# Bucketed attention into a rational feed-forward layer: sums and bits moved to stand ahead of a pair's first values product, and the other steps of a pair put at new places

## The chip, the cores and the metric

One core of one Trainium2 chip runs the whole program in one launch. The metric is the device time of that core in microseconds (us).

## The reference

Attention over 4 batches x 8 heads, 768 tokens, 64 wide, in which a query sees only the keys of its own bucket (six sign bits of a projection); then a feed-forward layer with a rational activation over the 3072 tokens of 512 features. All data is float32.

```python
q_bits = (einsum('bhsd,dk->bhsk', q, proj) > 0)           # k_bits likewise
mask = q_bucket[:, :, :, None] == k_bucket[:, :, None, :]
scores = np.where(mask, scale * q @ k.T, -1e9)
attn = exp(scores - max(scores)); attn = attn / (sum(attn) + 1e-09)
x = (attn @ v)  ->  [3072, 512]
h = x @ w_in                                              # [3072, 2048]
g = (a0 + a1*h + a2*h**2 + a3*h**3) / (1 + |b0|*|h| + |b1|*h**2 + 1e-6)
out = g @ w_out
```

## The kernel before

The 32 heads are worked in 16 pairs (NPAIR), p = 0 to 15; a pair stands on 128 partitions, two heads of 64. A product at near-float32 precision is made from two float32r matmuls: an operand is split into a rounded high part and the rest, the low part. After the pairs comes the feed-forward layer (`Ffn`), from about 406 us to the end, which the change hardly touches.

A pair has these steps; the name in brackets is that of its tile, as the profile and the order print it.

- `high`, `low` (q, k; lo): ScalarE rounds the operand, VectorE subtracts to get the low part. The low part has one buffer for q and one for k (`lo0`, `lo1`). `high_move`, `second_low` and `second_high` are SyncE's DMAs that lay the parts out for the scores.
- `bits` (psb): for two pairs at once, sixteen matmuls of 32 columns give the projections; VectorE takes the signs into `mb`, `penalties` scales them on ScalarE, `maskrows` moves them by four DMAs into spare rows of q and k, so that the scores' matmul itself adds the mask.
- `maxstep` (psm, m): for each of 12 blocks of rows a first product for the row maximum, two matmuls of 384 columns, which VectorE reduces. There are two PSUM buffers for it, which `bits` also uses.
- `shift_turn` (pst, mt) and `shift_rows`: the maxima are transposed and moved into one more row of q.
- `scores(p, s)` (pss, E): step s = 0 to 11. For each of two heads two matmuls into one PSUM tile, and ScalarE's exp into E. There are seven buffers E and three PSUM buffers of tag `s`, which psu and pst also use, in turn. GpSimd adds the E of three steps into `acc`, of which there are five.
- `values(p, s)` (psv): E times v, 64 columns to a head, accumulated over six steps in one PSUM buffer of tag `v`, which `values_out` copies out by ScalarE (col, xo). In pairs 1 to 14 the products of six steps are issued as one group of 24 matmuls, twice in a pair; in pair 15 in groups of 8.
- `sums` (psu, sr): sixteen matmuls of 32 columns on the four `acc` give the row sums, ScalarE copies them; `sums_store` and `recips` bring them through DRAM.
- `weights(i)`: loads and splits a block of the layer's weights (wr, ws, wi_hi, wi_lo), one of w_in and one of w_out in every pair; `tokens.load` makes the layer's first input block.

The order is written out ahead of time: `at(p, s, f, ...)` puts a step at place 12 p + s, the plan is sorted by place, and the instructions are issued in that order; nothing reorders them later, so that each engine's queue follows it. Work for pair p + 2 runs during pair p. The places of the middle pairs stand in the table `MID`, those of pair 0 and of what leads to it in `FIRST`. A place sets the order only; the time comes from the queues. The maxima of pair p + 2 are spread from place `maxima` + `maxima_steps` of pair p on (from pair p's step 7 to step 6 of pair p + 1).

Of the kernel before, what the change touches and what calls it, by code (L numbers as in the profile page):

```python
# [25 lines left out]
NPAIR = B * NHP  # L26
# [12 lines left out]
ACCS = 5  # L39

MID = dict(
    group=6, group_ends=2, values=[0.66, 0.05], values_ends=1.3, values_out=3.5, maxima=7.17,
    maxima_steps=[0, 1.15, 1.73, 2.64, 3.32, 5.08, 5.86, 6.98, 8.0, 8.84, 10.26, 11.37], sums=14.65, sums_store=17.37,
    high=[-0.41, 1.19], low=[1.06, 3.35], bits=2.81, penalties=4.05, high_move=1.9, maskrows=5.61, second_low=-2.2,
    second_high=2.69, load_v=10.99, shift_turn=8.61, shift_rows=8.82, load=9.0, recips=[20.0, 22.0, 23.0],
    weights=[[1.44, 4.0, 4.1, 5.09, 5.49, 7.11, 9.5, 9.75, 17.5], [8.05, 10, 10.65, 11.5, 12.38, 14.29, 16.34, 19.32, 21.22]],
    weights_last=[0.5, 0.8, 1.0, 1.2],
)

FIRST = dict(  # L50
    maxima0=[-0.28, 0.26, 1.25, 2.5, 2.92, 4.02], maxima1=4.13, rate1=0.48, maxima2=9.7, rate2=0.76,
    high=[1.64, 5.08], low=[3.52, 5.72], bits=5.52, penalties=7.05, high_move=7.01, maskrows=8.53, second_low=-0.75,
    second_high=7.95, load_v=9.81, shift_turn=9.64, shift_rows=9.65, group=2,
    values=[1.25, 1.5, 1.2, 0.57, 0.5, 0.94], values_out=1.96, high1=[7.05, 7.28], low1=[13.35, 22.75],
    high_move1=16.35, load2=10.64, load3=4.45, penalties1=0.83, maskrows1=4.05, first_shift=5.33,
    weights=[[0.71, 3.21, 4.75, 6.91, 11.35, 16.66, 25.25, 30.08, 32.02], [7.34, 8.03, 10.23, 11.08, 12.57, 13.45, 14.88, 21.36, 28.13]],
)
# [33 lines left out]
def bucket_attention_then_rational_ffn(ctx, tc, qT, kT, v, proj, w_in, w_out, coef, consts, out):  # L91
# [55 lines left out]
    def operands_to_terms():  # L147
        early.close()
        ffn.terms_pool(right)

    last = attention(tc, nc, raw, ps_b, tail, tokens, early, operands_to_terms, ffn, load, QF, KF, v, w_in, w_out, wo_d, ident, cst,
                     ones, prj, wi_hi, wi_lo, x_d, s_d, r_d, coefficients)
    ffn.rest(ctx, last)
# [3 lines left out]
def attention(ctx, tc, nc, raw, ps_b, tail, tokens, early, operands_to_terms, ffn, load, QF, KF, v, w_in, w_out, wo_d, ident, cst, ones, prj,  # L157
# [210 lines left out]
    def recips(bb):  # L368
        n = 2 * NHP * S // P
        s = tail.tile([P, n], F32, tag="rs", name=f"rs{bb}")  # L370
        nc.sync.dma_start(s, s_d[bb].rearrange("h (x c) -> (h x) c", c=n))
        yield
        z = tail.tile([P, n], F32, tag="rz", name=f"rz{bb}")
        d = tail.tile([P, n], F32, tag="rd", name=f"rd{bb}")
        r = tail.tile([P, n], F32, tag="rr", name=f"rr{bb}")
        nc.vector.tensor_scalar(out=z, in0=s, scalar1=0.0, scalar2=S * TINY, op0=ALU.is_equal, op1=ALU.mult)
        nc.vector.tensor_scalar(out=d, in0=s, scalar1=0.0, scalar2=1e-9, op0=ALU.is_gt, op1=ALU.mult)
        nc.vector.tensor_tensor(out=d, in0=s, in1=d, op=ALU.add)
        nc.vector.tensor_tensor(out=d, in0=d, in1=z, op=ALU.add)
        nc.vector.reciprocal(out=r, in_=d)  # L380
        yield
        nc.sync.dma_start(r_d[bb].rearrange("h (x c) -> (h x) c", c=n), r)
        yield
# [45 lines left out]
    def at(p, s, f, *args):  # L429
        plan.setdefault(12 * p + s, []).append((f, args))  # L430

    def spread(p, steps, gen):
        for s in steps:
            at(p, s, lambda g: next(g, None), gen)

    for p in range(NPAIR):
        mid = 0 < p < NPAIR - 1
        n = MID["group"] if mid else FIRST["group"] if p == 0 else MID["group_ends"]
        for s in range(12):
            at(p, s, scores, p, s)  # L440

            if p > 1:
                at(p - 2, MID["maxima"] + MID["maxima_steps"][s] if p > 2 else FIRST["maxima2"] + FIRST["rate2"] * s, maxstep, p, s)
            if s % n == n - 1:
                for i in range(s - n + 1, s + 1):
                    at(p, s + (MID["values"][s // n] if mid else FIRST["values"][s // n] if p == 0 else MID["values_ends"]), values, p, i)
            if s % NT == NT - 1:
                at(p, s + (MID["values_out"] if mid else FIRST["values_out"] if p == 0 else MID["values_ends"]+0.01), values_out, p, s // NT)
        for hf in range(2):
            at(p, 6 * hf + 9, values_store, p, hf)  # L450
        if p < NPAIR - 1:
            at(p, MID["sums"], sums, p)
            at(p, MID["sums_store"], sums_store, p)
        if p > 1:
            for t in range(2):
                at(p - 2, (MID if p > 2 else FIRST)["high"][t], high, p, t)
                at(p - 2, (MID if p > 2 else FIRST)["low"][t], low, p, t)
            if p % 2 == 0:
                at(p - 2, (MID if p > 2 else FIRST)["bits"], bits, p)
                at(p - 2, (MID if p > 2 else FIRST)["penalties"], penalties, p)  # L460
            at(p - 2, (MID if p > 2 else FIRST)["high_move"], high_move, p)
            at(p - 2, (MID if p > 2 else FIRST)["maskrows"], maskrows, p)
        if p > 0:
            at(p - 1, (MID if p > 1 else FIRST)["second_low"], second_low, p)
            at(p - 1, (MID if p > 1 else FIRST)["second_high"], second_high, p)
            at(p - 1, (MID if p > 1 else FIRST)["load_v"], load_v, p)
            at(p - 1, (MID if p > 1 else FIRST)["shift_turn"], shift_turn, p)
            at(p - 1, (MID if p > 1 else FIRST)["shift_rows"], shift_rows, p)
        if p > 3:
            at(p - 4, MID["load"], load, p)  # L470
        if p % NHP == NHP - 1 and p + 1 < NPAIR:
            spread(p, MID["recips"], recips(p // NHP))
# [5 lines left out]
        spread(0, [o + x for x in w], weights(i))  # L478

    for c in range(2):  # L480
        spread(NPAIR - 2, [9 * c + x for x in (6, 10, 11, 12)], tokens.load(0, c))
    at(NPAIR - 1, 2, operands_to_terms)
    for f in range(3):
        at(NPAIR, 2 + f, ffn.step, f)
    at(NPAIR, 2.5, sums, NPAIR - 1)

    load_v(0)
    warm(12)
# [241 lines left out]
```

## Time and profile before

| what | value |
|---|---|
| median of three runs | 951.18 us (950.34 to 953.0) |
| the profiled execution | 951.47 us, of which the span of its instructions 949.7 us |
| granted clock of TensorE | 0.998 |
| busy in the span | PE 938.9, VectorE 860.3, ScalarE 679.6, GpSimd 450.4 us |
| of that from 62 to 370 us (pairs 2 to 13) | PE 308.0 of 308.0, VectorE 270.9, ScalarE 215.4, GpSimd 246.1 us |

The matmuls are pipelined: one of 384 columns is shown as some 340 ns long, while the next one starts about 175 ns after it. So two of them cover each other, and a PE that is shown as always busy can still have lost time; this is read from the starts of the matmuls, or from the pieces of the chain of waits, which do not overlap. A score step (four matmuls) takes 0.70 us there, a block of maxima (two) 0.35 us.

### The profile page before, as it was taken

The numbers are of one execution on the slowest core, as the hardware profiler recorded it, in microseconds if no ns is written. First come the engines' busy times: TensorE is split into PE (matmuls) and PEld (weight loads), VectorE is DVE, ScalarE is ACT, GpSimd is POOL, SyncE is SP. The second block draws the span as 40 slices with busy tenths as digits, with TensorE's granted clock in tenths as the row PEclk, the third lists the DMA queues.
The fourth block names the chain that finished last, engine by engine and source line by source line (L and its number), as shares of the span: only waits on it lengthen the run. The fifth ranks groups of instructions, "written<-read, shape, count | busy, mean of one in ns | idle before, by whom it ended". The sixth has DMA issues, their size and how long they took to land.

```text
span 949.7 us, 14854 instructions
## 1 busy us (share of the span) xinstructions
PE 938.9 (99%) x5067; PEld 752.7 (79%) x5067; DVE 860.3 (91%) x1206; ACT 679.6 (72%) x1418; POOL 450.4 (47%) x399
## 2 busy tenths in 40 slices
PE   9999999999999999999999999999999999999998
PEld 5576767676767676488998998998998998998996
DVE  6789889888988897589999999999999999999996
ACT  6467777777777776777777777777777777777775
POOL 4377878787878787832222222222222222222222
PEclk9999999999999999999999999999999999999999
DMA  7568877778778777455121021021011110210000
GB/s 223 143 181 245 223 224 225 223 224 224 225 223 223 225 191 212 131 212 201 42 67 35 1 67 35 1 67 35 13 58 32 58 43 1 67 34 1 34 1 34
DMA packets 49888, 111.65 MB, mean 118 GB/s; under 512 B 9138, under 2 KB 21798, under 8 KB 49812
## 3 DMA queue, kind: packets, MB, share of 16 engines
q1 hardware_dynamic: 49524, 110.60, 39.5%
q8 instruction: 40, 0.66, 0.3%
q14 instruction: 36, 0.29, 0.1%
q10 hardware_dynamic: 288, 0.10, 0.1%
HBM read 56.82 MB, written 21.17 MB: 82 GB/s over the span
## 4 chain that ended last, share of the span: by engine, by line
PE 96%; DMA 1%; ACT 1%; DVE 1%; issue 0%; SPq 0%; ACTq 0%
PE psh L80 28%; PE pso L80 28%; PE pss L80 15%; PE psv L80 14%; PE psm L80 7%; PE psu L80 2%; PE psb L80 1%; DMA kf<-kT 0%; DVE c L80 0%; DMA q<-mb 0%; PE pst L80 0%; ACT E L80 0%; DMA k<-lo 0%; PE psw L80 0%; SPq L80 0%
## 5 line engine op out<-in xcount | busy, mean ns | idle before, releaser
L80 POOL TENSOR_TENSOR gl<-c,gh 128x384 fp32r<-128x384 f32 x128 | 140.8, 1100 | 393.8 <-ACT gh L80 367.3
L80 ACT ACTIVATE E<-pss 128x384 f32<-128x384 f32 x384 | 167.9, 492 | 113.7 <-PE pss L80 92.6
L80 PE MATMUL pso<-wo,gh 128*128 128x512 f32 x768 | 241.1, 395 | 0.0
L80 DVE TENSOR_REDUCE m<-psm 128x1 f32<-128x768 f32 x192 | 180.4, 950 | 40.9 <-PE psm L80 37.1
L80 POOL TENSOR_TENSOR acc<-E,E 128x384 f32<-128x384 f32 x128 | 162.4, 1289 | 82.8 <-ACT E L80 82.6
L80 PE MATMUL pss<-q,k 128*128 128x384 f32 (+2 forms) x768 | 173.4, 348 | 0.9 <-ACT E L80 0.5
L80 PE MATMUL psh<-xl,wi_hi 128*128 128x384 f32 x512 | 172.1, 336 | 0.0
L80 PE MATMUL psh<-xh,wi_hi 128*128 128x384 f32 x512 | 171.7, 335 | 0.0
L80 PE MATMUL psh<-xh,wi_lo 128*128 128x384 f32 x512 | 171.5, 335 | 0.0
L80 PEld LDWEIGHTS pso<-wo,gh 128*128 128x128 f32 x768 | 142.9, 188 | 23.7
L80 PEld LDWEIGHTS pss<-q,k 128*128 128x128 f32 (+2 forms) x768 | 134.7, 190 | 33.1 <-issue 19.8
L80 PE MATMUL pso<-wo,gl 128*128 128x512 f32 x384 | 152.2, 396 | 0.3 <-POOL gl L80 0.3
L80 ACT ACTIVATE h<-psh 128x384 f32<-128x384 f32 x128 | 63.1, 493 | 123.7 <-PE psh L80 123.7
L80 DVE SCALAR_TENSOR_TENSOR c<-c,ab,r 128x384 f32<-128x384 f32 x128 | 147.1, 1149 | 0.0
L80 POOL TENSOR_TENSOR acc<-acc,E 128x384 f32<-128x384 f32 x128 | 143.7, 1143 | 5.4 <-ACT E L80 5.4
L80 PE MATMUL psv<-E,v 128*64 128x385 f32 x768 | 133.9, 495 | 1.8 <-ACT xo L80 1.8
L80 PE MATMUL psm<-k,q 76*128 76x384 f32 (+1 forms) x384 | 102.3, 349 | 2.9 <-DMA q<-mb 2.3
L80 PEld LDWEIGHTS psv<-E,v 128*64 128x64 f32 x768 | 51.8, 137 | 66.6 <-issue 63.1
L80 PEld LDWEIGHTS psh<-xh,wi_hi 128*128 128x128 f32 x512 | 96.1, 188 | 6.3 <-ACT w L80 0.6
L80 PEld LDWEIGHTS psh<-xl,wi_hi 128*128 128x128 f32 x512 | 96.0, 188 | 5.1
L80 PEld LDWEIGHTS psh<-xh,wi_lo 128*128 128x128 f32 x512 | 96.1, 188 | 0.0
L80 ACT ACTIVATE c<-psh,ab 128x384 f32<-128x384 f32 x128 | 86.5, 676 | 1.7 <-POOL gl L80 1.7
(74 smaller groups left out, 1276.9 us busy)
## 6 DMA issues: line engine op xcount, KB each, us to landing
q<-q SPq DMA_DIRECT2D x45, 192.0 KB
k<-k SPq DMA_DIRECT2D x45, 192.0 KB
wr<-w_in SPq DMA_DIRECT2D x16, 512.0 KB
wr<-w_out SPq DMA_DIRECT2D x16, 512.0 KB
wo_d<-wr SPq DMA_DIRECT2D x16, 512.0 KB
wo<-wo_d SPq DMA_DIRECT2D x16, 512.0 KB
qf<-qT SPq DMA_DIRECT2D x16, 384.0 KB
kf<-kT SPq DMA_DIRECT2D x16, 384.0 KB
```

The costliest lines, as they stand in the source:

```text
L80: return self.tc.keep_in_program_order(issue(*args, **kwargs))
```

## The change

Three things are edited besides the numbers of `MID`. The sums of pair p and, every second pair, the bits of the pairs p + 3 and p + 4 get a place that is tied to that of the first values of pair p + 1, just ahead of them. The last pair's sums are issued one step of the layer later. The second half of `tokens.load(0, c)` has its last steps later. All other places in `MID` get new numbers; the kinds and sizes of the instructions stay as they are.

```diff
 MID = dict(
-    ... values=[0.66, 0.05], values_out=3.5, maxima=7.17, sums=14.65, high=[-0.41, 1.19], low=[1.06, 3.35], second_low=-2.2, ...
+    ... values=[0.42, 0.62], values_out=0.97, maxima=7.8, high=[-1.0, -0.44], low=[5.31, 4.54], second_low=1.16, ...
...
-            at(p, MID["sums"], sums, p)
+            at(p, 16.98 + MID["values"][0] if p < NPAIR - 2 else 16.28, sums, p)
...
-                at(p - 2, (MID if p > 2 else FIRST)["bits"], bits, p)
+                at(p - 2, 4.97 + MID["values"][0] if p > 2 else FIRST["bits"], bits, p)
...
-        spread(NPAIR - 2, [9 * c + x for x in (6, 10, 11, 12)], tokens.load(0, c))
+        spread(NPAIR - 2, [9 * c + x for x in (6, 10, 11 + c, 12 + c / 2)], tokens.load(0, c))
...
-    at(NPAIR, 2.5, sums, NPAIR - 1)
+    at(NPAIR, 3.5, sums, NPAIR - 1)
```

How it moves the instructions is seen in three places. In the order's names the pair's number comes first, then the step, the head and a running number: pss8_5_1 is pair 8, step 5, second head.

PE's queue, the sums of pair 7 in pair 8. Before, they follow the block of maxima after score step 2 (psm9_7), with the bits behind them, and then score step 3:

```order
L80 MATMUL psm9_7_2618<-k1_9_2331,q1_9_2299 128x384 x2
L80 MATMUL psu7_2627<-acc7_0_0_2322,ones_82 32x384 x2
L80 MATMUL psu7_2627<-acc7_1_0_2461,ones_82 32x384 x2
L80 MATMUL psu7_2627<-acc7_0_1_2395,ones_82 32x384 x2
L80 MATMUL psu7_2627<-acc7_1_1_2533,ones_82 32x384 x2
L80 MATMUL psb10_0_2643<-qf10_2240,prj_74 32x384
L80 MATMUL psb10_0_2643<-kf10_2242,prj_74 32x384
L80 MATMUL psb10_0_2643<-qf11_2510,prj_74 32x384
L80 MATMUL psb10_0_2643<-kf11_2512,prj_74 32x384
```

After, they follow the bits (the first row is the last of these) and the first values of pair 8 follow them:

```order
L81 MATMUL psb10_0_2674<-kf11_2543,prj_74 32x384
L81 MATMUL psu7_2684<-acc7_0_0_2324,ones_82 32x384 x2
L81 MATMUL psu7_2684<-acc7_1_0_2459,ones_82 32x384 x2
L81 MATMUL psu7_2684<-acc7_0_1_2376,ones_82 32x384 x2
L81 MATMUL psu7_2684<-acc7_1_1_2520,ones_82 32x384 x2
L81 MATMUL psv8_0_2697<-E5_153,v_8_2505 64x385 x2
L81 MATMUL psv8_0_2697<-E6_154,v_8_2505 64x385 x2
```

The sums and bits stood alone between score steps, and now stand in one run with psv; the block psm9_10 follows that run.

PE's queue, score steps 4 and 5 of pair 8. Before, a block of maxima stands between them:

```order
L80 MATMUL pss8_4_0_2668<-q1_8_2017,k1_8_2049 128x384
L80 MATMUL pss8_4_0_2668<-q2_8_2245,k2_8_2246 128x384
L80 MATMUL pss8_4_1_2672<-q1_8_2017,k1_8_2049 128x384
L80 MATMUL pss8_4_1_2672<-q2_8_2245,k2_8_2246 128x384
L80 MATMUL psm9_9_2680<-k1_9_2331,q1_9_2299 128x384 x2
L80 MATMUL pss8_5_0_2688<-q1_8_2017,k1_8_2049 128x384
L80 MATMUL pss8_5_0_2688<-q2_8_2245,k2_8_2246 128x384
L80 MATMUL pss8_5_1_2692<-q1_8_2017,k1_8_2049 128x384
L80 MATMUL pss8_5_1_2692<-q2_8_2245,k2_8_2246 128x384
```

After, the two steps follow each other, and the block stands behind both:

```order
L81 MATMUL pss8_4_0_2638<-q1_8_1987,k1_8_1999 128x384
L81 MATMUL pss8_4_0_2638<-q2_8_2327,k2_8_2328 128x384
L81 MATMUL pss8_4_1_2642<-q1_8_1987,k1_8_1999 128x384
L81 MATMUL pss8_4_1_2642<-q2_8_2327,k2_8_2328 128x384
L81 MATMUL pss8_5_0_2656<-q1_8_1987,k1_8_1999 128x384
L81 MATMUL pss8_5_0_2656<-q2_8_2327,k2_8_2328 128x384
L81 MATMUL pss8_5_1_2660<-q1_8_1987,k1_8_1999 128x384
L81 MATMUL pss8_5_1_2660<-q2_8_2327,k2_8_2328 128x384
L81 MATMUL psm9_9_2669<-k1_9_2281,q1_9_2269 128x384 x2
```

The same happens to steps 6 and 7 and to steps 8 and 9, so that three times in each of the pairs 2 to 13 eight matmuls pss stand together; in pair 1 once (steps 8 and 9). Before, no two steps of these pairs stood together.

ScalarE's queue from pair 14 to pair 15. Before, the last values of pair 14 are copied out (col14_1, xo14_1) behind the exps of three score steps:

```order
L80 ACTIVATE E5_153<-pss15_0_0_4476 128x384
L80 ACTIVATE E5_153<-pss15_0_1_4480 128x384
L80 ACTIVATE E6_154<-pss15_1_0_4486 128x384
L80 ACTIVATE E6_154<-pss15_1_1_4490 128x384
L80 ACTIVATE E0_148<-pss15_2_0_4500 128x384
L80 ACTIVATE E0_148<-pss15_2_1_4504 128x384
L80 CAST wr29_4410<-ws29_4411 128x512
L80 COPY col14_1_4520<-psv14_1_4462 128x1
L80 ACTIVATE xo14_1_4521<-psv14_1_4462,col14_1_4520 128x384
L80 COPY sr14_4533<-psu14_4524 128x384
```

After, this copy stands ahead of them:

```order
L81 ACTIVATE wr29_4403<-wr29_4403 128x512
L81 COPY col14_1_4476<-psv14_1_4462 128x1
L81 ACTIVATE xo14_1_4477<-psv14_1_4462,col14_1_4476 128x384
L81 ACTIVATE E5_153<-pss15_0_0_4480 128x384
L81 ACTIVATE E5_153<-pss15_0_1_4484 128x384
L81 ACTIVATE E6_154<-pss15_1_0_4490 128x384
L81 ACTIVATE E6_154<-pss15_1_1_4494 128x384
L81 CAST wr29_4403<-ws29_4404 128x512
L81 ACTIVATE E0_148<-pss15_2_0_4502 128x384
L81 ACTIVATE E0_148<-pss15_2_1_4506 128x384
```

On PE the group psv15_0, which uses the same PSUM buffer, follows score step 2 of pair 15 in both; it is followed by the sums of pair 14 before, and by score step 3 after.

More of the change, by code (lines that the diff above doesn't have):

```diff
@@ L41 @@
 MID = dict(
[L42 to L47, printed above, removed]
+    group=6, values=[0.42, 0.62], values_out=0.97, maxima=7.8,
+    maxima_steps=[-0.3, 1.22, 1.79, 2.72, 3.75, 4.38, 5.85, 6.72, 8.1, 9.54, 10.19, 11.45], sums_store=19.22,
+    penalties=5.61, high_move=0.36, maskrows=6.18, second_low=1.16, second_high=4.04, load_v=9.42, shift_turn=9.1,
+    shift_rows=9.54, recips=[21.54, 23.96, 32.05],
+    weights=[[3.46, 5.06, 5.4, 5.94, 6.84, 8.82, 10.79, 17.84, 19.97], [7.35, 10.09, 11.48, 11.93, 12.02, 13.53, 16.97, 19.12, 28.06]],
+    weights_last=[0.5, 0.8, 1.0, 1.2], values_ends=1.3, group_ends=2, high=[-1.0, -0.44], low=[5.31, 4.54],
+    load=11.46,
 )
```

## The prediction

> **What bounds the kernel now.** I read the busy times first, then the busy time by stretches, then who waited for whom on PE.
>
> ```profile
> PE 938.9 (99%) x5067; PEld 752.7 (79%) x5067; DVE 860.3 (91%) x1206; ACT 679.6 (72%) x1418; POOL 450.4 (47%) x399
> ...
> 62.00:370.00 308.00, 308.00 (x1881) 213.68 (x1879) 270.85 (x319) 215.43 (x486) 246.07 (x208) 1.00 0.78 219
> 370.00:407.00 37.00, 34.53 (x188) 18.93 (x185) 22.61 (x22) 24.80 (x58) 30.17 (x26) 1.00 0.44 139
> ...
> PE psv L80 <- ACT xo L80: 1.8, 1, 1.8
> ```
>
> The second part gives, for each stretch, the busy time of PE, weight loads, VectorE, ScalarE and GpSimd. In pairs 2 to 13 (62 to 370 us) PE is busy in all of 308.00 us at full clock, so nothing there shortens the program but fewer or closer matmuls, and whatever delays a matmul adds its whole length. The last row is the one long wait of PE after that, of psv for xo, 1.8 us, in pair 15.
>
> So the question is what PE pays between matmuls. The chain of waits gives start, length and count of each piece, without overlap; the rows up to 374.64 are from pair 14, the others from pair 15:
>
> ```profile
> 364.20 0.35 PE psm L80 x2
> 364.56 1.43 PE psu L80 x16
> 365.98 0.91 PE pss L80 x4
> ...
> 367.24 0.70 PE pss L80 x4
> ...
> 369.35 4.03 PE psv L80 x24
> 373.38 0.90 PE pss L80 x4
> ...
> 374.64 1.62 PE pss L80 x8
> ...
> 389.65 1.43 PE psu L80 x16
> 391.08 1.81 PE pss L80 x8
> 392.89 1.44 PE psv L80 x8
> 394.33 1.76 PE pss L80 x8
> ...
> 397.53 1.26 PE pss L80 x6
> ...
> 398.81 0.62 PE pss L80 x2
> 399.44 1.44 PE psv L80 x8
> 400.88 1.82 PE pss L80 x8
> ```
>
> Two prices stand here. A score step takes 0.70 us, but 0.90 or 0.91 behind a run of narrow matmuls (psu, psv): leaving such a run costs 0.21 us. And eight pss in a row take 1.62 us instead of 2 x 0.70: a second score step directly behind the first costs about 0.21 us too (1.62 less 1.41 by the starts).
>
> **The change part by part.** First, the merged runs. A lone psu group costs 1.43 + 0.21 us. At 389.65 it stood right behind a psv group of eight and took 1.43, and a psv group of eight takes 1.44 wherever it stands: the move from 64 to 32 columns costs as much as leaving does inside a group's own length, and the 0.21 is paid once for both. In the changed order the groups psu0 to psu13 (six of them with bits) lose their own exit: 14 x 0.21 = 2.9 us off. The nearest row has psv ahead of psu, the change has psu ahead of psv; I take the same price. The ends: no saving at all if this direction costs an exit more, and the length of psu ahead of psb if it costs nothing:
>
> ```profile
> 222.11 1.50 PE L80 MATMUL psu<-acc,ones 128*32 128x384 f32 x16
> 223.43 0.49 PE L80 MATMUL psb<-qf,prj 128*32 128x384 f32 x2
> ```
>
> Here psu begins 1.32 us ahead of psb, not 1.43; so at most 14 x 0.11 = 1.5 us more comes off.
>
> The Trainium skill says in TensorEngine Tiling (Array Packing), section Key Properties, that changing the tiling mode, not just the tile, drains TensorE. By that rule 32 to 64 columns pays like 64 to 32, and the sum stays; the row at 389.65 agrees for the one direction that the trace shows.
>
> Second, the score steps that now follow each other. Why the pair costs 0.21 us is seen in pair 14, where steps 7 and 8 stood together (the only case there with nothing odd around it):
>
> ```profile
> 374.48 1.78 PE L80 MATMUL pss<-q,k 77*128 77x384 f32 x8
> ...
> 375.64 0.30 PEld L80 LDWEIGHTS pss<-q,k 77*128 77x128 f32 x2 [0.25 <-ACT E L80]
> ...
> 375.09 0.87 ACT L80 ACTIVATE E<-pss 128x384 f32<-128x384 f32 x2 [0.19 <-PE pss L80]
> 234.79 0.62 ACT L80 CAST wi_hi<-ws 128x512 fp32r<-128x512 f32 x1
> 235.30 0.88 ACT L80 ACTIVATE E<-pss 128x384 f32<-128x384 f32 x2
> ```
>
> The fourth of the four score tiles needs the PSUM buffer of the first, as there are three. ScalarE starts on the first 0.61 us after its matmul began (374.48 to 375.09) and needs 0.49 for one; the weights of the fourth load at +1.16, where 1.06 was due for the matmul itself, and that load isn't hidden. ScalarE was free here, so this is the undisturbed price. With a block of maxima between the steps (0.35 us) the buffer is free in time, which is why pairs 2 to 13 show no such wait. The changed order has 3 x 12 + 1 = 37 such places: 37 x 0.21 = 7.8 us on. The bounds come from the four eights of pair 15, with the exit of 0.20 taken off: 1.76 - 1.60 = 0.16 (394.33), 0.21, 0.22, and 1.88 - 1.60 = 0.28 (397.53 with what follows it): 5.9 to 10.4 us. In pairs 14 and 15 such neighbours stand in both orders, three against four and as many; I count no difference.
>
> Third, behind steps 8 and 9: the cast wi_hi sits between their exps on ScalarE and takes 0.51 us of its time (234.79 to 235.30), so that the exps of step 9 come late, and step 10's first tile, which waits for one, has its weights loaded about 0.1 us too late, partly in cover. I take 0.07 us in 12 pairs, 0.8 us on; ends 0 and 12 x 0.21 = 2.5.
>
> Fourth, the end of the attention. Before, psv15_0 waits for xo14_1, which stands behind six exps and a cast:
>
> ```profile
> 386.78 0.63 ACT wr L80
> 387.41 0.07 ACT col L80
> 387.50 0.59 ACT xo L80
> ...
> 388.13 1.51 PE psv L80 x8
> ```
>
> Now the copy comes first, needs some 0.7 us right behind psv14_1, and the 1.8 us wait falls away; the exps start some 0.2 us later for it, which three score steps in a row feel. I take 1.6 us off (ends 0.8 and 1.9). The last sums, one step later, find their acc ready: a psu group there took 1.59 instead of 1.43, so 0.16 off. The later tokens.load stays ahead of the layer by some 2 us and costs nothing.
>
> Fifth, all that is only moved. GpSimd's acc of score step 4 needs a buffer that psu frees, now some 2.5 us later in every pair; it is idle 62 of 308 us, some 5 us in each pair, which covers that, and E of step 4 is used again only at step 11. On SyncE the moves of lo now stand behind those of q and k and are asked for later, on ScalarE the copies of q and k stand under the second psv group (4.03 us) with col and xo behind them. The tightest chain is that of the mask rows, in the six pairs with bits:
>
> ```profile
> 225.02 1.02 DVE L80 TENSOR_SCALAR mb<-psb,cst 128x768 fp32r<-128x768 f32 x1 [0.75 <-PE psb L80]
> 227.07 0.95 DVE L80 TENSOR_TENSOR lo<-kf,k 128x768 fp32r<-128x768 f32 x1
> 227.94 0.95 DVE L80 TENSOR_REDUCE m<-psm 128x1 f32<-128x768 f32 x1
> 229.14 1.50 DVE L80 TENSOR_TENSOR wr<-ws,wr 128x512 fp32r<-128x512 f32 x1
> 227.94 0.94 ACT L80 ACTIVATE mb<-mb,cst 128x768 fp32r<-128x768 f32 x1
> 228.90 0.79 SPq L80 DMA_DIRECT2D q<-mb  x1
> 229.74 0.80 SPq L80 DMA_DIRECT2D k<-mb  x1
> ...
> 234.13 0.52 PE L80 MATMUL psm<-k,q 76*128 76x384 f32 x2
> ```
>
> Before, the k row was asked for at 229.74 and its first user ran at 234.13 without a wait, so 4.4 us are enough. Now, counted from the first psb: VectorE has two reductions and two lo (0.87 each, 227.07 to 227.94) and one wr (1.5) ahead of mb. The first reduction belongs to the block two score steps and a block earlier (0.35 + 1.62 + 0.35 + 0.1 for the entry = 2.4 us ahead) and starts, by my estimate, 0.6 us behind it, as the exps do behind their tile: at -1.8. So VectorE comes to mb at 3.2 and ends at 4.2, ScalarE ends at 5.1, and the k row is asked for at 5.9, one q row later. The first user stands behind psb and psu (2.7), psv (4.0), two blocks and the exit (0.9) and two score steps (1.6), at 9.2 to 9.3: 3.4 us are left where 4.4 were enough and less may be. I take nothing; the upper end is 6 x 1.0 = 6 us.
>
> The sum, against the profiled execution's own 951.47 us: - 2.9 + 7.8 + 0.8 - 1.6 - 0.2 = + 3.9, or 955.3. That execution lay 0.3 us above the median of 951.18, so the forecast is 955.0 us.
>
> **The rivals.** Faster: the neighbouring score steps cost nothing, because ScalarE frees the first buffer in time. It decides if the release comes by about +0.88 us, a load of 0.18 ahead of the due +1.06, so that the weights stay hidden; the case followed above says +1.16, and none of the five eights shown took less than 0.16 more. Then 951.2 - 2.9 - 1.6 - 0.2 = 946.5 us. Chance 0.09.
>
> Same: 32 to 64 columns is free, as psu ahead of psb is, or the neighbours cost only 0.16: 955.0 - 1.5 = 953.5, or 955.0 - 1.9 = 953.1, both together 951.6 us. Against it stand the 1.43 at 389.65 and four of five eights. Chance 0.23.
>
> Slower still: a queue that is now tight runs over. Either the mask rows land late, as above (half the upper end gives 958 us), or ScalarE stands at the head of its queue for a weight load.
>
> ```profile
> 196.82 0.54 SPq L80 DMA_DIRECT2D wr<-w_in  x1
> ...
> 203.63 0.68 ACT L80 ACTIVATE ws<-wr 128x512 f32<-128x512 f32 x1 [0.53 <-DMA wr<-w_in]
> ```
>
> This load took 6.8 us. It is now asked for behind the store of xo, which ends 0.8 us into the pair with some 0.9 of issue, so about 1.7 us in; it lands 8.5 us in, while ScalarE comes to it at about 7: it stands still for 1.5 us, with the copy of psu, wr, mb and col behind it. These have until the end of psv (six score steps 4.2, five blocks 1.75, exit and eight 0.4, psu 1.43, psv 4.03: 11.8 us, 13.1 with bits) and need 1.6 to 2.6: some 1.8 us are left, and each us beyond that costs 12 us in all. Chance of either 0.15, at 958 to 961 us.
>
> The Trainium skill says in TensorE: Matmul & The Clock Gate, section Architectural detail, that ScalarE's queue is strict first in, first out; the wait of 0.53 us in the row above agrees, and it is by this rule that a late load would hold the exps.
>
> **How the numbers follow.** The base case has the remaining 0.53, its own range 953 to 957, a quarter of it below 954.0. About 0.3% (2.9 us) is what a measurement of this kernel can tell from no change, so the borders are 948.3 and 954.0 us. Slower: 0.40 + 0.15 = 0.55. Same: 0.13 + 0.23 = 0.36. Faster 0.09. The range leaves out the faster rival and the far end of the late queues: 950.5 to 960.0 us.
>
> **What would show it.** Right: in pairs 2 to 13 the chain has eights of pss at 1.6 us or more, with ScalarE's E as releaser of weight loads; psu, psv together one run with one exit of 0.2; psv15_0 without its wait for xo. Wrong: eights of 1.41 us; a psv behind psu shorter than 4.03; waits of psm for q<-mb or k<-mb at the first block of a new pair's maxima; ScalarE waiting for wr and PE for ScalarE right behind psv.

## The result, and the profile after

The changed kernel takes 958.7 us (median of five executions, 957.55 to 960.34) against 951.66 for the kernel before beside it: ratio 1.0071, 95% interval 1.0053 to 1.0088. It is slower by 7 us, 0.7%. The forecast was 955.0, with a range to 960.0. The ratios below leave out two executions at a lower granted clock, one of 1529.24 us at 0.557 (blocks apart, load earlier) and one of 983.53 us at 0.984 (merged, load earlier). The profiled execution took 957.55 us, 6.1 above that of before.

The busy times (time, share of the span, instructions), then the stretches of the pairs 2 to 13 and 14 to 15 (columns as before: PE, weight loads, VectorE, ScalarE, GpSimd):

```profile
PE 945.4 (99%) x5067; PEld 749.0 (78%) x5067; DVE 861.5 (90%) x1206; ACT 686.1 (72%) x1418; POOL 418.8 (44%) x399
```

```profile
62.00:370.00 308.00, 306.47 (x1824) 203.25 (x1821) 265.02 (x313) 216.44 (x472) 211.84 (x203) 1.00 0.76 214
370.00:407.00 37.00, 36.58 (x208) 21.65 (x207) 23.31 (x23) 26.95 (x62) 28.35 (x26) 1.00 0.64 182
```

Same clock, and PE is still busy nearly throughout: 306.47 of 308.00, with 1824 matmuls recorded in the window instead of 1881. So the loss is again between matmuls, in pieces too short for a row of waits. Who was waited for, PE first, then the weight loads (us in total, times, longest):

```profile
PE psm L81 <- DVE m L81: 1.5, 2, 1.2
...
PEld pss L81 <- ACT E L81: 17.6, 77, 0.5
```

PE's wait for xo is gone. Score weight loads waited for ScalarE's E 77 times; before it was 12 times, 4.1 us. ScalarE itself stood for its weight load (ws for wr<-w_in) once in each of the pairs 0 to 13, 39.3 us in all where it was 2.9 us before. The chain of waits shows pair 13 from its sums on, then two pieces of pair 15 and the last sums:

```profile
352.10 1.43 PE psu L81 x16
353.53 4.03 PE psv L81 x24
357.56 0.55 PE psm L81 x2
358.11 1.62 PE pss L81 x8
...
360.43 1.55 PE pss L81 x8
...
362.32 0.11 PE pst L81
362.44 0.35 PE psm L81 x2
362.78 0.86 PE pss L81 x4
...
364.00 0.87 PE pss L81 x4
...
393.24 1.39 PE pss L81 x6
394.62 1.45 PE psv L81 x8
...
417.31 1.43 PE psu L81 x16
```

psu and psv stand in one run with one exit (0.55 for a block of 0.35), psv keeps its 4.03 us. The neighbours take 1.62 and, where the cast wi_hi stands between their exps, 1.55. The single steps 10 and 11 take 0.86 and 0.87 where 0.70 was usual; the weight loads of both waited for exps (weight loads of pair 13 in order of time):

```profile
362.64 0.68 PEld L81 LDWEIGHTS pss<-q,k 77*128 77x128 f32 x4 [0.17 <-ACT E L81]
...
363.90 0.65 PEld L81 LDWEIGHTS pss<-q,k 77*128 77x128 f32 x4 [0.23 <-ACT E L81]
```

psv15_0 (394.62) follows its score steps at once, and the last sums take 1.43.

The same chain of the kernel before has, behind pst in pair 13, one piece that the prediction didn't see:

```profile
353.79 0.50 PE psm L80 x2
```

That block takes 0.35 now (362.44), 0.15 us less in every pair.

By the starts of their first score matmuls, pair 2 began 0.07 us later than before, pair 14 8.08 us later, the feed-forward layer 6.44, and the last matmul 6.06. So the twelve pairs 2 to 13 lost 8.0 us, of which 1.35 once, in pair 8. That place in the time order of VectorE, SyncE and PE (start, length, what; in brackets the idle time before it):

```profile
229.50 0.96 DVE L81 TENSOR_TENSOR lo<-kf,k 128x768 fp32r<-128x768 f32 x1 [1.97 <-DMA k<-lo]
...
233.53 1.00 DVE L81 TENSOR_SCALAR mb<-psb,cst 128x768 fp32r<-128x768 f32 x1
236.07 0.94 DVE L81 TENSOR_REDUCE m<-psm 128x1 f32<-128x768 f32 x1
```

```profile
236.38 0.83 SPq L81 DMA_DIRECT2D k<-mb  x1
```

```profile
237.27 0.52 PE L81 MATMUL psm<-k,q 76*128 76x384 f32 x2
238.97 0.41 PE L81 MATMUL psm<-k,q 76*128 76x384 f32 x1 [1.19 <-DVE m L81]
```

lo waited 2 us until the move out of its one buffer had ended, mb came late behind it, and the k row of the mask was asked for at 236.38, 14.4 us into the pair; in the five other pairs with bits it was 12.1 to 12.9. Its first user, the block at 238.97, ran 2.6 us later. The profile names m, but by the order the block needs the buffer that the reduction at 236.07 had left at 237.0; so I read it as the wait for the mask row. The semaphores in the trace bear this out: the last update of this transfer's semaphore is at 238.73, and PE's instruction that waits for it, ahead of the block's weight load, ends at 238.81.

### The profile page after: what moved, and what is told of

Read it like the earlier page. It is cut to its first block, busy times and chain, and to the rows that moved or that the text cites. A ratio compares the mean times of both kernels' runs of the same rounds, so it can differ in the third digit from the quotient of the medians.

```text
span 955.7 us, 14844 instructions
## 1 busy us (share of the span) xinstructions
PE 945.4 (99%) x5067; PEld 749.0 (78%) x5067; DVE 861.5 (90%) x1206; ACT 686.1 (72%) x1418; POOL 418.8 (44%) x399
## 4 chain that ended last, share of the span: by engine, by line
PE 95%; DMA 2%; DVE 2%; ACT 1%; issue 0%; SPq 0%; ACTq 0%
PE psh L81 28%; PE pso L81 27%; PE pss L81 15%; PE psv L81 13%; PE psm L81 7%; PE psu L81 2%; DMA wr<-w_in 1%; PE psb L81 1%; PE psw L81 1%; DMA q<-mb 0%; DVE c L81 0%; PE pst L81 0%; ACT E L81 0%; DVE m L81 0%; DVE ws L81 0%
## 5 line engine op out<-in xcount | busy, mean ns | idle before, releaser
L81 POOL TENSOR_TENSOR acc<-E,E 128x384 f32<-128x384 f32 x128 | 140.6, 1119 | 117.0 <-ACT E L81 89.6
L81 PE MATMUL pss<-q,k 128*128 128x384 f32 (+2 forms) x768 | 175.6, 355 | 0.7 <-DVE mt L81 0.4
L81 PEld LDWEIGHTS pss<-q,k 128*128 128x128 f32 (+2 forms) x768 | 130.8, 190 | 32.9 <-ACT E L81 17.6
L81 POOL TENSOR_TENSOR acc<-acc,E 128x384 f32<-128x384 f32 x128 | 133.2, 1061 | 8.5 <-ACT E L81 8.4
```

The source lines that it names most:

```text
L81: return self.tc.keep_in_program_order(issue(*args, **kwargs))
```

## The experiments

All ratios are to the kernel before on the same chip, with a 95% interval.

One reading is needed for several of them. In some traces the granted clock of TensorE falls to 0.5 for 3.41 us or for two or three times that, during a wait of PE or within 2.6 us behind one. The matmuls of scores and maxima then start 0.32 us after each other instead of 0.18, so that a wait costs more than its own length; I call this the half clock. It doesn't follow every wait, and what decides is not shown. The kernel before and the changed one have one such stretch each, at 28 us, and none in the pairs 2 to 15.

**What neighbouring score steps cost.** The kernel before, with the blocks of maxima put so that steps 4 and 5, 6 and 7, 8 and 9 stand together as in the change, and nothing else of it:

```diff
-    maxima_steps=[0, 1.15, 1.73, 2.64, 3.32, ..., 8.84, 10.26, 11.37], ...
-    shift_turn=8.61, shift_rows=8.82,
+    maxima_steps=[0.12, 1.85, 1.9, 3.0, 3.86, ..., 9.85, 10.26, 11.9], ...
+    shift_turn=9.05, shift_rows=9.1,
```

> The kernel before, with only the maxima moved so that score steps 4 and 5, 6 and 7, 8 and 9 follow each other in the pairs 2 to 13; sums and bits stay alone. Theory A: 36 x 0.21 = 7.6 us on, up to 3.6 more behind steps 8 and 9: 959 to 963 us. Rival B: the neighbours are covered by slack elsewhere: 951 to 953 us.

964.41 us, ratio 1.0106 (1.0086 to 1.0125). Its chain of waits, of one pair:

```profile
205.46 1.61 PE pss L80 x8
...
211.82 1.80 PE pss L80 x8
...
214.33 1.55 PE pss L80 x8
...
216.69 1.00 PE pss L80 x4
...
218.05 0.88 PE pss L80 x4
```

The eights cost 0.20, 0.20 (behind psv, so less an exit) and 0.14 us. That is the prediction's price. But the steps 10 and 11 cost 0.30 and 0.18 more, nearly as much as the eights. The pairs 2 to 13 lost 0.9 us each.

The other way round, the changed kernel with a block between all score steps:

```diff
-    maxima_steps=[-0.3, 1.22, 1.79, ..., 8.1, 9.54, 10.19, 11.45]
+    maxima_steps=[-0.3, 0.7, 1.79, ..., 8.1, 8.7, 10.19, 10.9]
```

> The changed order, with a block of maxima put back between score steps 4 and 5, 6 and 7, 8 and 9 of the pairs 2 to 13 (three numbers of the table); the merged runs and all other places stay. Theory A, that the neighbouring score steps cost the time: 36 x 0.21 = 7.6 us come off, and with them what steps 10 and 11 lose behind steps 8 and 9 in the trace of the changed kernel (about 0.3 us in each of 12 pairs, 3.6 us): from 958.7 to 948 to 951 us, below the kernel before. Rival B, that the later places of the lo moves, the weight loads and the bits cost it: 957 to 959 us, and PE then waits for VectorE or DMA where it waited for ScalarE.

963.04 us, ratio 1.0095 (1.007 to 1.0121): slower than with the neighbours. As a test of the neighbours' price it failed, since other waits took their place: PE waited 3.5 us for mask rows and 4.4 us for VectorE. Upstream ScalarE stood at the head of its queue for a load of weights, in the pairs 0 to 13:

```profile
ACT ws L81 <- DMA wr<-w_in: 50.7, 14, 4.2
```

The changed kernel has this wait too, but in 11 of the pairs 1 to 13 ScalarE was idle again, for 0.1 to 2.1 us, before it copied psv; here that is so in four. So the next kernel asks for that load earlier, and moves two transfers of q and k:

```diff
-    high_move=0.36, second_low=1.16, weights=[[3.46, 5.06, ...
+    high_move=1.3, second_low=0.3, weights=[[0.8, 5.06, ...
```

> The changed order with the blocks put back between the neighbouring score steps (as in the run where they stood apart), and in addition the moves of lo ahead of those of q and k, and the w_in load ahead of both (places 0.3, 1.3 and 0.8). In the trace of the run before this one ScalarE stood still 3.6 us for that load and VectorE behind it, and PE then waited for VectorE's reductions. Theory L, that these late transfers hold it: the waits of ScalarE for wr and of PE for m go, 947 to 950 us where the kernel before takes 951.7, a ratio of 0.995 to 0.998. Theory V, that VectorE has no room in this order wherever the transfers stand, since the sums and bits no longer give it time between the blocks: the ratio stays at 1.005 or more.

954.16 us, ratio 1.0019 (1.0002 to 1.0036). The late transfers had held the one before: 0.0076 of the ratio, 7 us, went with three numbers. This is also faster than the changed kernel with its neighbours (1.0071). But the terms of the prediction would give 947, without neighbours. The trace is of one more execution, on another chip:

> The same kernel as e5_apart_early (the changed kernel with blocks of maxima between all score steps and three transfers asked for earlier), for its trace: at 954 us it is 7 us above what the prediction's terms give without neighbours (951.5 less 2.9 less 1.6 = 947). If the steps 10 and 11 behind the cast wi_hi are the rest, they show 0.25 to 0.3 us in each of 12 pairs (3 to 3.6 us); if late transfers remain, there are waits of psm or psv for a DMA or of ScalarE for wr of over 1 us in several pairs.

954.04 us. From 62 to 400 us no wait of PE for a DMA is left. Steps 10 and 11 of one pair, by the chain of waits:

```profile
188.86 0.96 PE pss L81 x4
...
190.18 0.71 PE pss L81 x4
```

Step 11 is free again, step 10 is not: by the starts of its matmuls it took 0.1 to 0.35 us more in each of the twelve pairs, 2.5 us in all. The rest are waits of psm for VectorE, 4.1 us in seven places. The longest, in pair 9 (chain of waits):

```profile
254.24 1.68 DVE lo L81
...
258.45 0.96 DVE m L81
...
259.41 0.59 PE psm L81 x2
```

lo and the weights' steps stand under the first psv here and run into the next blocks, which come every 1.06 us. So one guess for the rest was right in kind and somewhat too large, and VectorE, in neither guess, is the larger part: 4.1 and 2.5 of 7. Late transfers hold PE no longer by themselves, but may still have a share in this: ScalarE waited for the load of w_in in seven places, and the two longest of these waits (2.9 and 2.6 us, pairs 9 and 10) stand ahead of the two longest waits of psm (1.6 and 0.7 us).

**The copy ahead of pair 15.** The changed kernel with only the last copy of pair 14 back behind three score steps:

```diff
-at(p, s + (MID["values_out"] if mid else ...
+at(p, s + (3.5 if p == NPAIR - 2 and s == 11 else MID["values_out"] if mid else ...
```

> The changed kernel, with only the copy of pair 14's second values put back behind the exps of pair 15's first three score steps. Theory A: the wait of psv15_0 for it comes back, 1.6 to 1.9 us on: 960.3 to 960.6 us. Rival B: the stretch was bound by something else and the time stays at 958.7 us.

962.75 us, ratio 1.0099 (1.0072 to 1.0127). PE's wait of psv for xo is back (2.0 us), and the chain shows that it isn't all:

```profile
404.18 5.27 DMA wr<-w_in
...
411.13 0.63 PE pss L81 x2
```

The store of xo stands ahead of the weight load on SyncE; with the copy late, the load was asked for late, and E behind ws held the score steps: some 1.5 us more (gaps of 0.95 and 0.58 on PE). Behind it the granted clock was 0.5 for 3.41 us, and the psv group at 413.15 took 2.76 us where 1.44 is usual. So pair 15, up to the layer, took 25.98 us against 20.99. The profiled execution lost another 5.8 us against the changed kernel in pair 2, which the edit doesn't touch: PE waited 1.4 us for a mask row there, and the granted clock was 0.5 for 10.24 us, which is some 5 us. The median's excess over the changed kernel is therefore no measure of the copy alone.

The clean test is the kernel before with this copy early (and the last sums one step later):

```diff
+at(p, s + (0.97 if p == NPAIR - 2 and s == 11 else MID["values_out"] if mid else ...
-    at(NPAIR, 2.5, sums, NPAIR - 1)
+    at(NPAIR, 3.5, sums, NPAIR - 1)
```

> The kernel before, with only the copy of pair 14's second values ahead of the exps of pair 15, and the last sums one step of the layer later. The fourth term of the prediction alone: 1.6 to 2.0 us and 0.2 us off, a ratio of 0.998. Rival: the wait comes back at the next exps, ratio 1.000.

949.72 us, ratio 0.9962 (0.9947 to 0.9978): 3.6 us less by the ratio, and faster than both kernels. Its chain of waits has psv15_0 directly behind step 2:

```profile
385.04 1.39 PE pss L80 x6
386.43 1.44 PE psv L80 x8
```

Pair 15 and what follows it up to the layer took 20.98 us (22.76 before), 1.8 less, as in the changed kernel (20.99). Other traces show where more can come from. Five kernels have the late copy in the old order: the kernel before, neighbours, merged, and the two with less work for VectorE. Three of them have the granted clock at 0.5 for 3.41 us right behind the wait for xo, and pair 15 took 24.2 to 24.4 us in these:

```profile
390.14 2.72 PE psu L80 x16
```

That is the psu of 1.43 us, in the kernel before with less work for VectorE. With the early copy none of seven traces has it (20.9 to 21.1 us). So the wait costs 1.8 us in some executions and 3.4 in others. How often is not known, so the share of this in the 3.6 us stays open.

All copies early, `values_out=0.97` for the pairs 1 to 14:

> The kernel before with all copies of psv out (col, xo) directly behind their values group, in pairs 1 to 14; nothing is merged and no score steps are neighbours. Theory: only the wait in pair 15 counts (1.6 to 1.8 us off), the others have cover: ratio 0.996 to 0.999. Rival: in each of 24 groups the exps start 0.2 us later for the copy, which the next score steps feel: up to 24 x 0.2 = 4.8 us on, ratio 1.000 to 1.004.

950.06 us, ratio 0.9964 (0.9945 to 0.9982). The pairs 2 to 13 took as long as before (by starts within 0.3 us), so only the last copy counts, and moving the others is free in the old order.

**What the merged runs bring.** The kernel before with sums and bits merged into one run ahead of psv, and only what hangs on them moved along:

```diff
-    ... sums_store=17.37, ... bits=2.81, penalties=4.05, ... maskrows=5.61, ... weights=[[1.44, 4.0, 4.1, 5.09, 5.49, ...
+    ... sums_store=17.9, ... bits=5.63, penalties=5.64, ... maskrows=5.65, ... weights=[[1.44, 4.0, 4.1, 5.67, 5.68, ...
...
-            at(p, MID["sums"], sums, p)
+            at(p, 17.65 if p < NPAIR - 2 else MID["sums"], sums, p)
```

> The kernel before, with only the sums and bits moved ahead of the first values (and, so that the mask rows are still in time, their scaling and moves put directly behind them and two VectorE steps of the weights put behind the bits). Theory A: 13 to 14 exits of 0.21 us are saved, 2.7 to 2.9 us off: 948.8 us against 951.7. Rival B: the bits come too late at this place, the first block of the next pair's maxima waits in the six pairs with bits, and the time is that of before or 1 to 6 us more.

979.35 us, ratio 1.0257 (1.0235 to 1.028). Exits of 0.21 were saved and 25 us lost. Its waits:

```profile
PE pss L80 <- ACT E L80: 7.1, 13, 0.7
...
PE psb L80 <- DVE m L80: 3.0, 6, 0.8
```

Not all of the loss is waits. In the stretch of the pairs 2 to 13 the granted clock (third figure from the end) is 0.97:

```profile
62.00:370.00 308.00, 296.80 (x1717) 197.58 (x1714) 246.09 (x294) 200.18 (x446) 220.14 (x191) 0.97 0.71 202
```

It was 0.5 for 6.83, 3.41 and 6.83 us in the pairs 2, 5 and 9, each time behind or between waits of PE, and these pairs took 4.1, 1.9 and 3.6 us more than their like: 9.6 of the 26 us that the pairs 2 to 13 lost in this trace. Over all executions the mean clock is 0.990, against 0.997 for the kernel before, so by my estimate (time x missing clock) it makes some 7 of the 25 us. In the next merged kernels it is 5 and 8 us by the same estimate.

Is VectorE too full? The next takes two of its steps per weight block away, those that join high and low words, in the merged and in the old order:

> The kernel before with the sums and bits merged (as in the run that took 2.6% more), without the two VectorE steps that put a weight block's high and low words together (so the weights are wrong), some 4.3 us of VectorE's time in a pair. To be compared with the kernel before without the same steps. Theory V, that the merged order loses its time because VectorE gets no room between the blocks of maxima: the difference to that kernel falls from + 25 us to between - 3 and + 3 us. Rival M, that the mask rows come too late, or GpSimd's sums: it stays over + 10 us.

> The kernel before without the same two VectorE steps (the weights are wrong). PE was busy all the time from pair 2 to pair 13, so nothing is to be won: 950 to 952 us, a ratio of 0.998 to 1.000, by every theory.

975.93 us, 1.0231 (1.0206 to 1.0256), and 952.51 us, 0.9988 (0.9974 to 1.0002). So the amount of VectorE's work is not it. The timelines of ScalarE and PE of the first show a place whose wait comes 13 times from 62 to 400 us:

```profile
162.93 0.58 ACT L80 ACTIVATE xo<-psv,col 128x384 f32<-128x384 f32 x1
163.41 1.75 ACT L80 ACTIVATE E<-pss 128x384 f32<-128x384 f32 x4
```

```profile
163.95 0.62 PE L80 MATMUL pss<-q,k 77*128 77x384 f32 x2 [0.63 <-ACT E L80]
```

Behind a cast of k and one of wr, col and xo push the exps back until a score step waits. In the old order, as I read it, ScalarE worked this off under the lone sums. So: casts and copies directly behind psv, where ScalarE is free, and the weight load earlier:

```diff
+    values_out=0.97, high=[-1.0, -0.44], weights=[[0.8, ...
```

> The kernel before with sums and bits merged ahead of the first values (as in e2_merged), and besides with ScalarE's casts of q and k and its copies of psv placed directly behind a values group, where it has nothing else to do, and one load asked for earlier. Theory S (ScalarE's place): merged runs alone lost because the lone sums group had been the 1.4 us in which ScalarE worked off the cast of k, wr, col and xo between the exps; without it the fourth or fifth score step of a pair waits for an exp. Then pss' waits for ACT E (7 us in the two kernels without this) fall below 2 us, and the time comes to the kernel before less 2.9 (exits) less 1.6 (last copy) plus 0 to 6 us for the waits of psm and psb for VectorE's m: ratio 0.995 to 1.002. Rival theory B (buffers): psm and psb share two buffers, and GpSimd's acc waits for psu, which now comes later; these are unchanged here, so the ratio stays at 1.02 or more.

974.94 us, 1.0262 (1.0224 to 1.0299): no better, though the waits for E are all gone from its profiled execution (its fastest, 968.70 us):

```profile
PE psm L80 <- DVE m L80: 6.3, 11, 2.7
PE psb L80 <- DVE m L80: 5.5, 6, 1.0
```

VectorE and PE of one of its pairs:

```profile
210.94 0.95 DVE L80 TENSOR_TENSOR lo<-qf,q 128x768 fp32r<-128x768 f32 x1
211.81 1.82 DVE L80 TENSOR_REDUCE m<-psm 128x1 f32<-128x768 f32 x2
```

```profile
212.82 0.62 PE L80 MATMUL psm<-k,q 76*128 76x384 f32 x2 [0.34 <-DVE m L80]
```

Blocks come every 1.06 us and a reduction takes 0.87; one lo between two of them makes a later block wait, and the bits stand for the same buffers. It is not how much VectorE has to do in a pair but where. The last kernel moves lo, and an even block of weights, behind the merged run:

```diff
-    low=[1.06, 3.35], weights=[[0.8, 4.0, 4.1, 5.67, 5.68, ...
+    low=[5.642, 5.645], weights=[[0.8, 5.68, 5.69, 5.7, 5.71, ...
```

> As e12_merged_early, and VectorE's two lo and ScalarE's and VectorE's steps on an even block of weights besides moved from between the score steps to behind the merged run of bits, sums and first values. Theory V: with the lone sums gone, twelve blocks of maxima follow each other every 1.06 us, of which VectorE needs 0.87, so that any lo (0.87) between them makes the next block wait; in e12_merged_early this cost 0.6 us in each pair (psm for m) and about 1 us more in each pair with bits (psb for m). Then psm's and psb's waits for m (11.8 us in e12_merged_early) fall below 4 us and the time comes to 948 to 955 us, a ratio of 0.995 to 1.003. Rival theory D: merged runs lose by transfers that are asked for too late (w_in's load, lo's moves, mask rows); these get no earlier here, so that waits for DMAs stay or grow and the ratio stays above 1.015.

954.83 us, ratio 1.001 (0.9996 to 1.0023): 0.025 of the ratio, 24 us, are back. The waits of PE for m from 62 to 400 us are down from 11.8 us to

```profile
PE psm L80 <- DVE m L80: 0.5, 3, 0.2
```

So the place of the other engines' work was the cause (theory V); steps of ScalarE on the weights moved along with VectorE's, so the shares of the two are not told apart. With the waits the half clock went too: the mean clock is 0.9985 again, so by the same estimate some 8 of the 24 us came back that way. Yet nothing is left of the merge's saving: each of the pairs 2 to 13 still takes 0.5 us more than before. The chain of waits of pair 13 shows where:

```profile
351.64 3.14 DVE lo L80 x2
354.79 1.15 DVE wr L80
...
358.03 1.74 DVE m L80 x2
...
359.82 0.62 PE psm L80 x2
```

From 351.64 to 358.03 VectorE is busy with lo and the weights, 6.4 us, where psu and psv give 5.5; by the starts of the matmuls two blocks of each pair come 0.2 to 0.3 us late. And lo has become longer than it was (groups by line from 62 to 370 us, the last numbers being busy us, mean ns of one and idle time; first before, then this kernel):

```profile
L80 DVE TENSOR_TENSOR lo<-kf,k 128x768 fp32r<-128x768 f32 x12 | 12.1, 1005 | 0.0
```

```profile
L80 DVE TENSOR_TENSOR lo<-kf,k 128x768 fp32r<-128x768 f32 x13 | 22.9, 1762 | 0.0
```

## Why the prediction was right, and where it was off

The sign and the range held, and the slower side, to which 0.55 was given. But 958.7 lies outside the base case's own 953 to 957, in the 958 to 961 us that were meant for the late queues. By the profiled executions + 6.1 us came where + 3.9 was worked out; that it stayed within 960.0 is in part luck, since one term ran over its own end and another loss stood in no term. Term by term, over the pairs 2 to 13 from the rows of pair 13 (12 times each):

| term | predicted | measured |
|---|---|---|
| merged runs, exit saved | - 0.21 a pair | - 0.21: one exit, psu 1.43, psv 4.03 |
| neighbours | + 0.63 a pair | + 0.56 (1.62, 1.62 as in other pairs, 1.55, less 3 x 1.41) |
| steps 10 and 11 | + 0.07 a pair, at most 0.21 | + 0.33 (0.86 + 0.87 - 1.40) |
| block behind pst | not seen | - 0.15 |
| sum of twelve pairs | + 5.9 | + 6.4; by the starts 8.0, with the 1.35 of pair 8 |
| psv15_0's wait for xo | - 1.6 | - 1.8 |
| last sums | - 0.2 | - 0.16 |

**Merged runs.** The move from 32 to 64 columns costs as much as that from 64 to 32: psv behind psu keeps 4.03 us. The Trainium skill says in TensorEngine Tiling (Array Packing), section Key Properties, that a change of mode drains TensorE; by that rule both directions pay, and the trace agrees with its 4.03.

**Neighbours.** Right in mechanism and size; the same lengths came back when they alone were put into the kernel before. The rival "faster" needed weight loads that stay hidden; 77 of them waited for E.

**Steps 10 and 11: the term that was mis-sized.** I followed the cast wi_hi to the first tile of step 10 and stopped there. Step 10 pays 0.16 us, not 0.07, and step 11 as much again: its first weight load (363.90) waited for the exp of step 10's first tile, which ran from 363.36 to 363.85. ScalarE had been idle for 0.39 us before that exp, so this is no backlog of ScalarE: the late step hands its delay on. Together it is 4.0 us instead of 0.8, beyond the end of 2.5. Moved alone, the neighbours brought it too (1.00 and 0.88); with the blocks back between them step 11 was free.

**Mask rows.** Costed at nothing, with 3.4 us between the asking and the user. Five pairs of six bear that out. In one, lo waited for its buffer, and 1.35 us were lost; this is the rival of late queues, at one place. Its other half came too, without a price on PE: ScalarE stood 1.2 to 4.2 us in each pair for the load of w_in, where 1.5 was worked out, and PE has no wait for ScalarE behind psv; in pair 13 ScalarE was idle again 0.68 us before the copy. The chain that I gave left out that lo's single buffer waits for a move, which now stands later on SyncE.

**What I had not weighed.** The saving is not free of the rest of the order. Merged in the old order, the sums bring no saving but 25 us of loss, some 7 of it by the half clock. That the loss went when the other engines' work was moved shows that the lone runs had been time in which they worked off what stands between the score steps. The changed order has other room for that, under psv and, as I read it, in the neighbours' missing blocks; it pays 0.56 + 0.33 us a pair for these and saves 0.21. The neighbours are not needed for it: with the blocks apart and three transfers earlier the ratio was 1.0019. But none of the merged kernels was faster than the kernel before.

## What to carry to other kernels

A gap on the bounding engine that costs 0.2 us can be the room in which two other engines catch up: before it is removed, count for each of them how much work stands between the pieces that remain, not only how busy it is over the stage. A score step that waits for an exp can pass the delay to the step behind it even if ScalarE is idle in between, so a cast put among exps is to be followed further than to the first tile that waits. A wait of PE can cost more than its length, if the granted clock falls behind it; read the clock of a stretch before its loss is put down to waits alone. And of a change that gains in one place and loses in many, take the one place alone: the early copy ahead of pair 15 brought 0.4% with two numbers.

## What the hardware showed

VectorE's lo of k, the same instruction on the same shape, took 1.00 us on average in the kernel before and 1.76 in the last one, where GpSimd's acc waits for the same psu. The Trainium skill says in SBUF — State Buffer, section SBUF: two separate sides, that a VectorE operation with two SBUF inputs and a GpSimd operation that reads SBUF hold one pair of ports exclusively, and that the one which starts first gets it. The traces agree in detail. Where lo of k begins during an acc that has 0.2 us or more to go, it ends 0.81 to 0.82 us after that acc, in 23 of 24 such cases in these three kernels. In the last kernel the acc had 0.94 to 0.95 us left in each pair, and lo took 1.75 to 1.77; in the changed kernel it had 0.54 to 0.67 left in five pairs (1.36 to 1.49), and nothing ran beside lo in five (0.96). In the kernel before lo began first in five pairs (0.95), or 0.26 to 0.28 us ahead of an acc's end in five (1.08 to 1.10); there the acc that began during lo was the one to wait, with 1.70 to 1.74 us where an acc without such a neighbour takes 0.86 to 1.03. No run was made for this; the pairs differ in it by themselves. It explains why work moved to a free stretch of VectorE doesn't fit there as its old length says.

The clock at 0.5 is the other fact. Beside the kernel before and the changed one, eleven traces have a mean clock of 0.989 or more; six of them have stretches at 0.5 behind pair 0, of 3.41, 6.83 or 10.24 us, and a psu of 1.43 us took 2.72 in one. In the merged kernel two waits of PE of 0.4 and 0.2 us, at 161.13 and 162.87, are all that stands ahead of the stretch at 163.07; the same waits at 367.37 and 369.10 were followed by none.
